# Transposing token chunks and DFT matrices by DMA instead of on TensorE

## The chip, the cores and the metric

The kernel runs on one core of a Trainium2 chip. The metric is device time in microseconds (us) of one execution; lower is better.

## What is computed

A long convolution (H3) is gated by the normalised input, and multiplied by an activated two-layer network of the same input. S = 2048 tokens, D = 640 channels, F = 1728 hidden units, all inputs bfloat16:

```python
x = A_q                                    # 2048 x 640
xn = layernorm(x)                          # no scale, no shift
k_shift = causal 4-tap convolution of A_k along the tokens, a filter per channel
kv = k_shift * A_v
y = irfft(rfft(pad(kv)) * rfft(pad(A_ssm_k)))[:2048]     # per channel
y = y + kv * A_ssm_D
s = xn * y
h = gelu(xn @ B_w1 + B_b1)                 # 2048 x 1728
g = silu(h @ B_w2 + B_b2)
out = x + s * g
```

## The kernel before

**Tokens.** Token 16 p + j lies on partition p, row j. The 16 rows are four chunks of four rows (512 tokens each). Each chunk of x is loaded into a tile `xn` of 128 x 4 x 640, normalised in place, and turned into `xnT`, with channels on the partitions (5 blocks of 128) and 512 tokens along the free dimension. There is one tile `xnT`, used by the four chunks in turn.

**Network.** `ffn1` (L376) makes one of 14 blocks of 128 hidden units for a chunk: five matmuls of 128 x 512 with a block of `w1_sb` stationary and `xnT` moving; `ffn1_out` applies gelu on ACT into `hT`. Steps h0 to h13 are the first chunk, h14 to h27 the second, h28 to h41 the third, h42 to h55 the fourth. `ffn2` (L394) takes a row of a chunk and half of the channels: 14 matmuls of 128 x 320; silu on ACT, and a product into `xn` on DVE. Steps g0 to g31.

**Convolution.** The transform along the tokens is done as matrix products in two factors. `WA` and `WB` (128 x 16 x 128) hold the forward matrices of the first factor, made by sines on ACT (L237); the small ones lie in `mats`. The filter goes through `k_tr` (L421), `k_f1` (kf) with WA and WB, a store to `scrK` in HBM, a load in another order (`kin_load`, fl) and `k_f2` (ff), into `Khat`. The taps and the product with v (`kv_step`, cv) run on DVE; the result goes through `u_f1` (uf), a store to `scrU`, a load (`uin_load`, ml) and `u_f2` (mu). Then come the product with Khat on DVE (`product`, mp), which also needs a half-swapped copy of Khat made by an on-chip DMA (`swap_load`, mk), the first inverse factor (`inv1`, mc), a store to `scrC`, a load (`cab_load`, yl), and the second inverse factor (`inv2`, y). `inv2` multiplies with `GA` and `GB`: `WA` and `WB` with each of their 16 blocks of 128 x 128 transposed. `gate` and `out_add` finish a row.

**The transposes.** The first chunk is transposed in the prologue, block by block on TensorE (L655 to L658), and copied from PSUM to `xnT` by three DVE copies and one of ACT (L659 to L661). The other three use steps `tt` (`x_tr`, L367) and `te` (`x_tr_out`, L373): one `tt` is four matmuls with the identity, one `te` one copy of 128 x 512 from PSUM on ACT or DVE. There are 15 pairs, tt5 to tt9 for the second chunk, tt10 to tt14 for the third, tt15 to tt19 for the fourth. The matrices use `it` (`i2_tr`, L488; eight blocks each, four steps) and `ie` (`i2_out`, L493). The PSUM tiles of `tt` are two buffers that they share with ffn1 and ffn2; those of `it` are three buffers shared with the rest of the convolution.

**Order.** The whole program after the prologue is a list written out in `PLAN` (L30 to L71), a step a word; the letter behind a dot is the engine of a copy (a for ACT, d for DVE). Each engine, and each DMA queue, runs its part of that list in order. Loads, and the swaps of Khat, are issued by SP; stores to scrK, scrU, scrC and most of the output by POOL. So a load on SP waits behind all earlier loads, and a wait of an earlier one holds it back too.

Places that the change touches, in the words of `PLAN` before:

```
... kc3.d kf5 ke5.a ks2 V2 tt7 te7.a kt5 kc5.d tt9 te9.a kt4 gm5 ... K2 tt8 te8.a ... tt5 te5.d tt6 te6.a uf1 kt7 ...
... fl11 uf26 ue26.a cv57 ... fl12 ff16 fe16.d ff17 fe17.a fl15 ff12 fe12.a tt12 te12.a ff14 ...
... mk15 h40 he40 mc21 ... h41 he41 te17.d mc24 ... ms7 q0 g17 ...
```

V and K load four rows of v and of k, q a chunk of x for the last addition.

Of the kernel before, what the change touches and what calls it, by code (L numbers as in the profile page):

```python
# [11 lines left out]
BF16 = mybir.dt.bfloat16  # L12
# [4 lines left out]
P = 128  # L17
# [4 lines left out]
DT = D // P  # L22
# [19 lines left out]
ke28.a h21 he21 uf6 ue6.a kf29 ke29.a ks14 uf7 ue7.a us3 h22 he22 h23 he23 kf26 ke26.a gm7 cv37 cv38 cv41 cv42
cv39 kf27 ke27.a ks13 kt15 kc15.d kf30 ke30.a kf31 ke31.a ks15 fl0 fl1 fl2 h24 he24 fl4 uf10 ue10.a gm6 ls15 ls8
ls9 uf8 ue8.a ls14 uf11 ue11.a us5 h25 he25 h26 he26 uf14 ue14.a cv43 ls13 lv3 lr3 h27 he27 cv44 ls11 lv2 lr2
cv45 cv46 cv47 uf12 ue12.a uf9 ue9.a us4 fl3 uf15 ue15.a us7 g8 ge8 gm8 ln13 ln9 uf13 ue13.a us6 fl5 g9 ge9 ff3
fe3.a ln12 ff1 fe1.d ln10 ff2 fe2.a cv56 ff0 fe0.a cv48 cv49 cv50 ln8 uf21 uf20 ue20.a ue21.a us10 ff8 fe8.a
ln11 g10 ge10 uf16 ue16.a ff6 fe6.d gm9 ff9 fe9.a fl7 ff5 fe5.a ff7 fe7.a fl9 ff4 fe4.a fl8 uf17 ue17.a us8 g11
ge11 cv51 cv52 cv53 cv54 cv55 ff11 fe11.a ff10 fe10.a fl6 uf18 ue18.d uf19 ue19.a us9 fl11 uf26 ue26.a cv57 cv58
cv59 uf24 ue24.a uf27 ue27.a us13 uf25 ue25.a us12 fl12 ff16 fe16.d ff17 fe17.a fl15 ff12 fe12.a tt12 te12.a
ff14 fe14.a cv60 cv61 cv62 cv63 ff18 fe18.a ff15 fe15.a fl13 g12 ff19 fe19.a fl10 uf22 ue22.d ff13 fe13.a fl14  # L50
uf31 gm11 ge12 uf30 ue30.a ue31.d us15 ff23 fe23.d gm12 uf23 ue23.a us11 gm10 tt14 te14.d uf29 uf28 ue28.d
ue29.a us14 mk0 ml0 ml1 mk1 mk2 mk3 ml2 ml3 ml5 ml4 ff31 fe31.a tt13 te13.a tt10 te10.d it0 ie0.d ff27 fe27.d
ff25 fe25.d g13 ge13 gm13 g14 ge14 gm14 ff29 fe29.d ln14 ff28 fe28.a ff24 fe24.d g15 ge15 gm15 ff21 fe21.a tt11
te11.d ff22 fe22.a mu0 mp0 ff26 fe26.a ml7 h28 he28 mu2 mp2 ml10 ml8 mu1 mp1 mk4 mc0 me0.a h29 he29 ff30 fe30.a
mu3 mp3 mk5 ml12 h30 he30 ml11 mc2 me2.a mu4 mp4 mc1 me1.a ms0 mu5 mp5 mk6 h31 he31 ml6 ff20 fe20.a mc3 me3.a
ms1 ln15 mu6 mp6 mc4 me4.a mu7 mp7 mk7 ml9 h32 he32 mu8 mp8 mc5 me5.a ms2 mc6 me6.a mu11 mp11 mc7 me7.a ms3 mu10
mp10 h33 he33 mu9 mp9 mk8 mk9 mc8 me8.a mc10 me10.a mu12 mp12 mu13 mp13 mk10 mc11 me11.a ms5 ml14 h34 he34 ml15
mc12 me12.a it1 ie1.d mc13 me13.a ms6 mu15 mp15 h35 he35 mu14 mp14 mk11 ml13 mc9 me9.a ms4 mu18 mp18 h36 he36
mc14 me14.a mu17 mp17 h37 he37 mu16 mp16 mk12 mc15 me15.a mu20 mp20 h38 he38 mu19 mp19 mk13 mc18 me18.a h39 he39
mu21 mp21 mk14 mc16 me16.a tt17 mc19 me19.a ms9 mc17 me17.a ms8 mu23 mp23 mc20 me20.a mu22 mp22 mk15 h40 he40  # L60
mc21 me21.a ms10 mu24 mp24 mu25 mp25 mc22 me22.a h41 he41 te17.d mc24 me24.a mu26 mp26 mc25 me25.a ms12 tt15
te15.a mu27 mp27 tt16 te16.d mc23 me23.a ms11 mc26 me26.a tt18 te18.d mu29 mp29 it3 ie3.a mu28 mp28 g16 ge16
gm16 mc27 me27.a ms13 it2 ie2.d tt19 te19.a mu31 mp31 mu30 mp30 ms7 q0 g17 ge17 gm17 mc28 me28.a mc31 mc29
me29.d ms14 mc30 me30.d me31.d ms15 yl5 yl2 yl0 yl4 yl3 yl1 yl6 yl11 yl15 q1 g18 ge18 gm18 g19 ge19 gm19 g20
ge20 gm20 g21 ge21 gm21 g22 ge22 gm22 g23 ge23 gm23 h42 he42 h43 he43 y0 yt0 yo0 h44 he44 h45 he45 h46 he46 y5
yt5 yl8 y4 yt4 yo4 yo5 ys2 y1 yt1 yo1 ys0 y3 yt3 h47 he47 h48 he48 h49 he49 h50 he50 h51 he51 y2 yt2 yl7 yl14
yl9 yl10 yl12 yo2 yo3 ys1 q2 h52 he52 h53 he53 h54 he54 h55 he55 y6 yt6 yl13 yo6 y7 yt7 yo7 ys3 q3 y8 yt8 yo8
y11 yt11 g24 ge24 g25 ge25 g26 y12 yt12 gm24 ge26 gm25 ga24 ga25 gs25 y15 yt15 g27 ge27 y14 yt14 y13 yt13 gm26
ga26 gm27 ga27 gs27 y9 yt9 yo9 ys4 y10 yt10 yo10 yo11 ys5 g28 ge28 gm28 ga28 g29 ge29 gm29 ga29 g30 ge30 gm30
ga30 gs30 g31 ge31 gm31 ga31 gs29 gs31  # L70
"""  # L71


# [1 line left out]
def kernel(  # L75
# [15 lines left out]
    nc = tc.nc  # L91

    CH = 4
# [15 lines left out]
    ffnp = ctx.enter_context(tc.tile_pool(name="ffnp", bufs=1))  # L109
# [23 lines left out]
    def evac(eng, out_ap, in_ap):  # L133
        if eng == "a":
            return nc.scalar.copy(out=out_ap, in_=in_ap)  # L135
        return nc.vector.tensor_copy(out=out_ap, in_=in_ap)

    w1_sb = wts.tile([P, DT, FT * P], BF16, name="w1_sb")
# [7 lines left out]
    ident = consts.tile([P, P], BF16, name="ident")  # L146
# [5 lines left out]
    WA = consts.tile([P, NJ, P], BF16, name="WA")  # L152
    WB = consts.tile([P, NJ, P], BF16, name="WB")
    GA = consts.tile([P, NJ, P], BF16, name="GA")
    GB = consts.tile([P, NJ, P], BF16, name="GB")
# [90 lines left out]
    sm = {}  # L246
# [62 lines left out]
                                 rhs=ident[:, h * 64:(h + 1) * 64], start=True, stop=True)  # L309
        return ps  # L310

    xnT = ffnp.tile([P, DT, CH * P], BF16, name="xnT")
    hT = ffnp.tile([P, FT, CH * P], BF16, name="hT")
    kvtmp = ep.tile([P, KC, D], BF16, name="kvtmp")
    live = {}
# [7 lines left out]
    def big_of(key, bf=False):  # L323
        return take(key, ps_big, [P, 1024] if bf else [P, 2, 512], BF16 if bf else F32, "big")

    def ffn_of(key, bf=False):
        return take(key, ps_ffn, [P, 1024] if bf else [P, 512], BF16 if bf else F32, "ffn")
# [36 lines left out]
        nc.vector.tensor_scalar(out=xr, in0=xr, scalar1=live["mv", c][:, j, 0:1], scalar2=live["rs", c][:, j:j + 1],  # L364
                                op0=ALU.subtract, op1=ALU.mult)

    def x_tr(i):  # L367
        c, t = divmod(i, DT)
        tp = ffn_of(("tt", i), True)
        for q in range(CH):  # L370
            nc.tensor.transpose(out=tp[:, q * P:(q + 1) * P], in_=xn_tiles[c][:, q, t * P:(t + 1) * P], identity=ident[:])

    def x_tr_out(i, eng):  # L373
        evac(eng, xnT[:, i % DT, :], live["tt", i][:, 0:CH * P])

    def ffn1(i):  # L376
        ft = i % FT
        ps = ffn_of(("h", i))
        for t in range(DT):
            nc.tensor.matmul(out=ps[:, :], lhsT=w1_sb[:, t, ft * P:(ft + 1) * P], rhs=xnT[:, t, :],  # L380
                             start=(t == 0), stop=(t == DT - 1))

    def ffn1_out(i):
# [101 lines left out]
    def k_f2_out(g, eng):  # L485
        cast(eng, Khat[:, g, :], live["ff", g])

    def i2_tr(i):  # L488
        tp = big_of(("it", i), True)
        for q in range(8):  # L490
            nc.tensor.transpose(out=tp[:, q * P:(q + 1) * P], in_=(WA, WB)[i // 2][:, i % 2 * 8 + q, :], identity=ident[:])

    def i2_out(i, eng):  # L493
        q4 = i % 2
        evac(eng, (GA, GB)[i // 2][:, q4 * 8:(q4 + 1) * 8, :].rearrange("p a b -> p (a b)"), live["it", i][:])

    def add_d():
        nc.vector.tensor_tensor(out=kf_sb[:, :, 0], in0=kf_sb[:, :, 0], in1=dD_sb[:], op=ALU.add)
# [74 lines left out]
    def prologue():  # L573
# [83 lines left out]
                    nc.tensor.transpose(out=tp_of[t][:, q * P:(q + 1) * P], in_=xn[:, q, t * P:(t + 1) * P],  # L657
                                        identity=ident[:])  # L658
        for t in range(DT - 2):  # L659
            evac("d", xnT[:, t, :], tp_of[t])  # L660
        evac("a", xnT[:, DT - 2:DT, :].rearrange("p a b -> p (a b)"), tps[DT - 2][:])  # L661

    steps = {
        "P": load_params, "pt": param_tr, "pb": param_out, "X": load_x, "A": load_w1, "B": load_w2, "C": load_kf, "K": load_k, "V": load_v,
        "ls": ln_stats, "lv": ln_eps, "lr": ln_root, "ln": ln_norm, "tt": x_tr, "te": x_tr_out,
        "h": ffn1, "he": ffn1_out, "g": ffn2, "ge": ffn2_silu, "gm": ffn2_mul, "ga": last_add, "gs": last_store,
        "w": f1_phase, "ws": f1_sines, "d": add_d, "em": tap3, "ee": tap3_out,
        "sp": small_iotas, "s": small_phase, "ss": small_sine, "sm": small_mats,
        "kt": k_tr, "kc": k_tr_out, "kf": k_f1, "ke": k_f1_out, "ks": k_store,
        "cv": kv_step, "uf": u_f1, "ue": u_f1_out, "us": u_store,  # L670
        "fl": kin_load, "ff": k_f2, "fe": k_f2_out, "it": i2_tr, "ie": i2_out,
        "ml": uin_load, "mk": swap_load, "mu": u_f2, "mp": product, "mc": inv1, "me": inv1_out, "ms": c_store,
        "q": xq_load, "yl": cab_load, "y": inv2, "yt": gate, "yo": out_add, "ys": out_store,
    }
# [35 lines left out]
```

## Time and profile before

| What | Value |
|---|---|
| runs | 229.15, 231.75 and 233.93 us, median 231.75 |
| profiled execution, first to last instruction | 231.0 us |
| its mean granted TensorE clock | 0.984 |
| TensorE (PE) busy | 211.6 us, 1420 matmuls |
| DVE, ACT, POOL busy | 184.1, 149.6, 43.1 us |
| DMA | 57.61 MB, 25209 packets |
| 60 matmuls and 15 copies of `tt`/`te` | PE 5.46, ACT 4.70, DVE 2.85 us busy |
| 32 matmuls and 4 copies of `it`/`ie` | PE 2.44, DVE 2.08, ACT 1.01 us busy |

The profile is of one execution; its own time, apart from the span, is not listed among the runs, and the span lies 0.75 us below their median. PE is TensorE's matmuls, PEld its weight loads, DVE VectorE, ACT ScalarE, POOL GpSimd, SP SyncE, which computes nothing here and issues DMAs. A row of a group gives line, engine, operation, output and inputs with shapes, and count; then busy us and mean ns of one; then the engine's idle time just before them. Matmuls overlap: one can last 219 ns while the next begins after 55 ns. The chain is the work that ended last, followed back from the end; its pieces have a start and a length in us. DMA issues are given with their size and the median time from issue to landing.

### The profile page before, as it was taken

Reading aid. Unit: us, or ns where it says so; the run is one execution under the profiler, and the core shown is the slowest. Engines: PE = TensorE matmul, PEld = TensorE weight load, DVE = VectorE, ACT = ScalarE, POOL = GpSimd, SP = SyncE. Lnnn points to the kernel's source line nnn. Section 1 sums busy time; section 2 is a strip of 40 time slices with the busy share of each in tenths; the row PEclk is TensorE's granted clock in tenths of the full one; section 3 lists DMA queues with packets and bytes.
Section 4 is the critical chain, followed back from the end, with each engine's and each line's share of the span. In section 5 each row is a group of like instructions: output and inputs, shape, how many; then the busy total and the mean of one; then the engine's idle time right before and its main releaser. Section 6 shows DMA issues by size and latency. Waiting matters only on the chain.

```text
span 231.0 us, 3921 instructions
## 1 busy us (share of the span) xinstructions
PE 211.6 (92%) x1420; PEld 131.7 (57%) x1420; DVE 184.1 (80%) x315; ACT 149.6 (65%) x232; POOL 43.1 (19%) x75
## 2 busy tenths in 40 slices
PE   7859999899999899979999965999999999999993
PEld 4524456677555556646765532556677765457772
DVE  7799999889989999999779885699998115444892
ACT  3934687998988999898468742567782244562111
POOL 8100020042232344120200220212222000100010
PEclk9988999999999999999999997999999999999999
DMA  7999995654844479599779999877943695379323
GB/s 219 349 380 355 409 413 206 191 209 174 305 191 188 179 236 381 176 309 337 266 215 294 303 353 295 257 231 188 270 156 131 207 340 200 150 218 367 124 89 114
DMA packets 25209, 57.61 MB, mean 249 GB/s; under 512 B 2854, under 2 KB 14055, under 8 KB 25190
## 3 DMA queue, kind: packets, MB, share of 16 engines
q1 hardware_dynamic: 20726, 39.66, 52.6%
q0 software_dynamic: 4320, 17.70, 20.5%
q8 instruction: 11, 0.18, 0.3%
q14 instruction: 8, 0.07, 0.1%
q10 hardware_dynamic: 144, 0.01, 0.0%
HBM read 33.76 MB, written 18.35 MB: 226 GB/s over the span
## 4 chain that ended last, share of the span: by engine, by line
PE 65%; ACT 12%; DMA 9%; DVE 8%; issue 3%; SPq 1%; DVEq 0%; ACTq 0%
PE g L399 22%; PE h L380 21%; ACT Khat L135 6%; DMA kh<-scrU 6%; PE uf L340 3%; PE mc L537 3%; DMA Khat<-Khat 3%; PE mc L538 2%; PE mu L340 2%; PE kf L340 2%; PE ff L340 2%; PE y L556 2%; PE y L557 2%; DMA skp<-in_A_shift_k_dram 1%; ACT sl L404 1%
## 5 line engine op out<-in xcount | busy, mean ns | idle before, releaser
L380 PE MATMUL h<-xnT,w_sb 128*128 128x512 bf16 x280 | 68.4, 390 | 1.5 <-ACT hT L386 1.2
L399 PE MATMUL g<-w_sb,hT 128*128 128x320 bf16 x448 | 63.7, 299 | 0.6 <-ACT sl L404 0.6
L386 ACT ACTIVATE hT<-h,b_f 128x512 bf16<-128x512 f32 (+1 forms) x56 | 38.3, 690 | 27.3 <-PE h L380 24.2
L399 PEld LDWEIGHTS <-hT 128*128 128x128 bf16 x448 | 43.8, 98 | 18.1 <-issue 0.8
L529 DVE TENSOR_TENSOR p<-mu,Khat 128x1280 bf16<-128x1280 f32 x32 | 45.8, 1484 | 5.4 <-PE mu L340 3.7
L380 PEld LDWEIGHTS <-w_sb 128*128 128x128 bf16 x280 | 27.9, 100 | 31.3 <-issue 4.6
L404 ACT ACTIVATE sl<-g 128x320 bf16<-128x320 f32 x32 | 13.9, 439 | 36.1 <-PE g L399 32.5
L135 ACT CAST c<-mc 128x640 bf16<-128x640 f32 x29 | 19.9, 692 | 8.6 <-PE mc L538 7.9
L544 POOL DMA_DIRECT2D scrC<-c x16 | 11.5, 718 | 56.0 <-ACT c L135 51.8
L409 DVE TENSOR_TENSOR xn<-xn,sl 128x320 bf16<-128x320 bf16 x32 | 10.1, 322 | 14.0 <-ACT sl L404 13.8
L472 DVE TENSOR_TENSOR uc<-uc,kvtmp 128x1280 bf16<-128x1280 bf16 x24 | 19.8, 824 | 0.7
L476 DVE TENSOR_TENSOR kvtmp<-kh,w_exp 128x1280 bf16<-128x1280 bf16 x24 | 19.7, 820 | 0.5
L340 PEld LDWEIGHTS <-mats 128*128 128x128 bf16 x128 | 12.1, 97 | 13.8 <-issue 4.9
L537 PE MATMUL mc<-p,mats 128*128 128x320 bf16 x64 | 18.6, 305 | 1.2 <-DVE p L529 0.7
L538 PE MATMUL mc<-p,mats 128*128 128x320 bf16 x64 | 18.5, 304 | 0.0
L563 DVE TENSOR_TENSOR t<-y,xn 128x640 bf16<-128x640 f32 x12 | 9.8, 820 | 10.4 <-PE y L557 10.3
L135 ACT CAST Khat<-uf 128x640 bf16<-128x640 f32 x26 | 17.0, 697 | 0.4 <-PE uf L340 0.4
L340 PE MATMUL mu<-kh,mats 128*128 128x320 bf16 x64 | 13.5, 300 | 3.7 <-DMA kh<-scrU 2.5
L135 ACT CAST Khat<-ff 128x640 bf16<-128x640 f32 x24 | 15.5, 699 | 0.5 <-PE ff L340 0.4
L135 ACT CAST Khat<-kf 128x640 bf16<-128x640 f32 x22 | 15.1, 711 | 0.3 <-PE kf L340 0.2
L440 POOL DMA_DIRECT2D scrK<-Khat x16 | 8.9, 554 | 31.2 <-ACT Khat L135 16.6
L340 PE MATMUL ff<-kin,mats 128*128 128x320 bf16 x64 | 12.3, 298 | 1.4 <-ACT Khat L135 1.3
(111 smaller groups left out, 269.4 us busy)
## 6 DMA issues: line engine op xcount, KB each, us to landing
scrK<-Khat POOLq DMA_DIRECT2D x16, 320.0 KB, 2.6
scrU<-Khat POOLq DMA_DIRECT2D x16, 320.0 KB, 4.2
kin<-scrK SPq DMA_DIRECT2D x16, 320.0 KB, 4.6
Khat<-Khat SPq DMA_DIRECT2D x32, 160.0 KB, 4.2
kh<-scrU SPq DMA_DIRECT2D x16, 320.0 KB, 5.4
scrC<-c POOLq DMA_DIRECT2D x16, 320.0 KB, 3.9
kh<-scrC SPq DMA_DIRECT2D x16, 320.0 KB, 6.2
kh<-in_A_k_dram SPq DMA_DIRECT2D x4, 640.0 KB, 6.1
```

What stands on the lines that cost most here:

```text
L135: return nc.scalar.copy(out=out_ap, in_=in_ap)
L340: nc.tensor.matmul(out=ps[:, h, 0:HALF], lhsT=lhsT, rhs=rhs[:, h * HALF:(h + 1) * HALF], start=start, stop=stop)
L380: nc.tensor.matmul(out=ps[:, :], lhsT=w1_sb[:, t, ft * P:(ft + 1) * P], rhs=xnT[:, t, :], start=(t == 0), stop=(t == DT - 1))
L386: nc.scalar.activation(out=hT[0:M, ft, :], in_=live["h", i][0:M, :], func=ACT.Gelu_apprx_tanh, bias=b1_f[0:M, ft:ft + 1], scale=1.0)
L399: nc.tensor.matmul(out=ps[:, 0:HALF], lhsT=hT[0:M, ft, q * P:(q + 1) * P], rhs=w2_sb[0:M, ft, hs], start=(ft == 0), stop=(ft == FT - 1))
L404: nc.scalar.activation(out=sl[:], in_=live["g", i][:, 0:HALF], func=ACT.Silu)
L472: nc.vector.tensor_tensor(out=uc[:], in0=uc[:], in1=kvtmp[:], op=ALU.add)
L476: nc.vector.tensor_tensor(out=(kvtmp if s else uc)[:], in0=kh[:, r0:r0 + KC, :], in1=w_exp[:, j:j + 1, :].to_broadcast([P, KC, D]), op=ALU ...
L529: nc.vector.tensor_tensor(out=p[:].rearrange("p k (h c) -> p k h c", h=2), in0=live["mu", g][:, None, :, 0:HALF].to_broadcast([P, 2, 2, HA ...
L537: nc.tensor.matmul(out=psC[:, h, 0:HALF], lhsT=I1a, rhs=p[:, 0, hs], start=True, stop=False)
L538: nc.tensor.matmul(out=psC[:, h, 0:HALF], lhsT=I1b, rhs=p[:, 1, hs], start=False, stop=True)
L544: nc.gpsimd.dma_start(out=pair_view(scrC)[g2], in_=live["c", g2][:])
```

## The change

Steps `tt`, `te`, `it` and `ie` are removed from `PLAN`, with their functions. Each of the second to fourth chunk is turned by one transposing DMA on SP (`xd1`, `xd2`, `xd3`), and each of the two matrices by one (`ig0`, `ig1`). The first chunk stays on TensorE. The two inner dimensions of `xnT` change places, since the DMA turns row after row: it is now 128 x 4 x 5 x 128 (row, block of channels, token), and ffn1 reads it in four runs of 128.

```diff
-    xnT = ffnp.tile([P, DT, CH * P], BF16, name="xnT")
+    xnT = ffnp.tile([P, CH, DT, P], BF16, name="xnT")
...
-    def x_tr(i):
-        c, t = divmod(i, DT)
-        tp = ffn_of(("tt", i), True)
-        for q in range(CH):
-            nc.tensor.transpose(out=tp[:, q * P:(q + 1) * P], in_=xn_tiles[c][:, q, t * P:(t + 1) * P], identity=ident[:])
-
-    def x_tr_out(i, eng):
-        evac(eng, xnT[:, i % DT, :], live["tt", i][:, 0:CH * P])
+    def x_turn(c):
+        nc.sync.dma_start_transpose(out=xnT[:].rearrange("p q t s -> p (q t) s"),
+                                    in_=xn_tiles[c][:].rearrange("p q d -> p (q d)"))
...
-            nc.tensor.matmul(out=ps[:, :], lhsT=w1_sb[:, t, ft * P:(ft + 1) * P], rhs=xnT[:, t, :],
+            nc.tensor.matmul(out=ps[:, :], lhsT=w1_sb[:, t, ft * P:(ft + 1) * P], rhs=xnT[:, :, t, :],
...
-    def i2_tr(i):
-        tp = big_of(("it", i), True)
-        for q in range(8):
-            nc.tensor.transpose(out=tp[:, q * P:(q + 1) * P], in_=(WA, WB)[i // 2][:, i % 2 * 8 + q, :], identity=ident[:])
-
-    def i2_out(i, eng):
-        q4 = i % 2
-        evac(eng, (GA, GB)[i // 2][:, q4 * 8:(q4 + 1) * 8, :].rearrange("p a b -> p (a b)"), live["it", i][:])
+    def i2_turn(i):
+        nc.sync.dma_start_transpose(out=(GA, GB)[i][:], in_=(WA, WB)[i][:].rearrange("p n r -> p (n r)"))
...
-            evac("d", xnT[:, t, :], tp_of[t])
-        evac("a", xnT[:, DT - 2:DT, :].rearrange("p a b -> p (a b)"), tps[DT - 2][:])
+            evac("d", xnT[:, :, t, :], tp_of[t].rearrange("p (q s) -> p q s", q=CH))
+        evac("a", xnT[:, :, DT - 2:DT, :].rearrange("p q t s -> p t q s"), tps[DT - 2][:].rearrange("p (t q s) -> p t q s", t=2, q=CH))
```

In `PLAN` the new steps stand here; the order of all others is as before:

```
... kc3.d kf5 ke5.a ks2 xd1 V2 kt5 kc5.d kt4 gm5 ...
... fl11 xd2 uf26 ue26.a cv57 ...
... mk15 ig0 ig1 h40 he40 mc21 ... h41 he41 xd3 mc24 ... ms7 q0 g17 ...
```

## Prediction

> **What bounds the kernel now.** I read the shares of the page first, then the busy times by stage, then the rows of the work that goes, then the chain of waits and the order of time around each place where a transposing DMA enters, and last the DMA rows.
>
> ```profile
> PE 211.6 (92%) x1420; PEld 131.7 (57%) x1420; DVE 184.1 (80%) x315; ACT 149.6 (65%) x232; POOL 43.1 (19%) x75
> PE 65%; ACT 12%; DMA 9%; DVE 8%; issue 3%; SPq 1%; DVEq 0%; ACTq 0%
> ```
>
> The first line is the busy time of each engine over the span, the second the chain that ended last, by engine. By stage:
>
> ```profile
> 44.00:57.00 13.00, 12.45 (x115) 9.52 (x115) 10.86 (x22) 12.26 (x23) 3.75 (x7) 1.00 0.60 220
> ...
> 100.00:120.00 20.00, 18.65 (x143) 12.59 (x141) 16.61 (x29) 13.98 (x25) 3.25 (x6) 1.00 0.83 276
> ...
> 133.00:143.00 10.00, 5.71 (x31) 3.04 (x30) 6.82 (x5) 3.28 (x5) 1.43 (x2) 0.95 1.05 339
> 143.00:163.00 20.00, 19.79 (x122) 11.40 (x120) 17.68 (x14) 12.79 (x19) 3.90 (x6) 0.94 0.80 231
> 163.00:176.00 13.00, 12.93 (x110) 9.35 (x109) 12.45 (x14) 9.46 (x14) 3.25 (x5) 1.00 0.63 206
> ```
>
> After the stretch (us from the start) the columns are its length, then the busy time of PE, PEld, DVE, ACT and POOL, the clock and the DMA share. PE is the bound over most of the span, and it is full from 143 on. ACT is nearly as full from 44 to 57. Only 133 to 143 leaves PE idle (5.71 of 10 us busy), and there the DMA share is 1.05: the kernel waits for loads.
>
> **What is removed.** These rows go:
>
> ```profile
> L371 PE MATMUL tt<-ident,xn 128*128 128x128 bf16 x60 | 5.5, 219 | 0.0
> L135 ACT COPY xnT<-tt 128x512 bf16<-128x512 bf16 x8 | 4.7, 609 | 0.0
> L136 DVE COPY xnT<-tt 128x512 bf16<-128x512 bf16 x7 | 2.8, 419 | 0.0
> L491 PE MATMUL it<-ident,WA 128*128 128x128 bf16 x16 | 1.2, 219 | 0.0
> ```
>
> 219 ns is the time of one matmul, but they overlap. What PE really gives is read from the chain, which counts each stretch once:
>
> ```profile
> 103.20 0.22 PE tt L371 x4
> ...
> 110.44 0.45 PE tt L371 x8
> 110.89 0.45 PE it L491 x8
> ...
> 118.93 1.19 ACT Khat L135 x2
> ...
> 126.99 5.86 DMA Khat<-Khat
> ```
>
> Four transposes are 0.22 us and eight of the DFT matrices 0.45 us. So 15 x 0.22 + 4 x 0.45 = 5.1 us of PE go, with 4.7 + 1.0 us of copies on ACT and 2.8 + 2.1 us on DVE. By place:
> - 44 to 57 (chunk 1): 5 x 0.22 = 1.1 us of PE and 2.34 us of four ACT copies, with both engines over 94% busy. The chain here changes between ACT and PE; I take 1.3 us, between the 1.1 of PE and the 2.3 of ACT.
> - 100 to 120 (chunk 2, and the first half of one matrix): the chain holds 0.22 + 0.22 + 0.45 + 0.45 = 1.3 us. All of that lies ahead of the DMA piece at 126.99, so the waiting stage moves forward as a whole. The fifth group, at 118.57, is not on the chain: nothing.
> - 143 to 176 (chunk 3, three matrix halves): PE is 32.7 of 33 us busy. 5 x 0.22 + 3 x 0.45 = 2.45 us of PE go; I take 2.2, as DVE (30.1 of 33) is close behind and loses 2.5 us of its own.
> Together 1.3 + 1.3 + 2.2 = 4.8 us, if all transposes are hidden.
>
> **What is added.** Five transposing DMAs on SP: three of 640 KB (20 blocks of 128x128) and two of 512 KB (16 blocks). Nothing is moved on POOL, and the order of the other instructions of each engine stays. No row of this trace shows a transposing DMA. These are the nearest ones (KB each, median us to landing):
>
> ```profile
> kh<-in_A_k_dram SPq DMA_DIRECT2D x4, 640.0 KB, 6.1
> vc<-in_A_v_dram SPq DMA_DIRECT2D x4, 640.0 KB, 7.7
> Khat<-Khat SPq DMA_DIRECT2D x32, 160.0 KB, 4.2
> q1 hardware_dynamic: 20726, 39.66, 52.6%
> ```
>
> Call t the time for which one 640 KB transpose holds SP and the transfers behind it, and t + 2.5 the time to landing; 2.5 us is the shortest landing of a 160 KB on-chip copy. From below, SP holds a plain issue for 0.33 to 0.6 us and 640 KB land in 6.1: t = 3.6. From above, each source row of a block (128 elements, 256 bytes) costs a packet of the mean length: 0.526 x 231 x 16 / 20726 = 94 ns, so 2560 x 94 ns / 16 = 15 us. I take t = 5.2, from the dearest plain load of the same size (7.7 - 2.5), the nearest row; a 16-block one costs 0.8 t. The ends 3.6 and 15 stay for the range.
>
> The Trainium skill has rules on both sides. Its page "Advanced Engine Details and Errata", section "X-Bar Transpose (TRN2)", says that transposing DMAs run about as fast as regular ones, which is near the lower end. Its page "VectorE: DVE Perf Modes", section "The three transpose paths", gives 1309 ns for one 128x128 block by DMA against 390 ns on TensorE, where this trace has about 55 ns (0.22 / 4) on TensorE. An estimate by that page, block after block, is 20 x 1.309 = 26 us for a chunk; no run here shows it yet.
>
> Now the three places.
> - Chunk 1. The DMA stands ahead of the third load of v and of k on SP and waits for the last normalisation:
>
> ```profile
> 45.80 0.44 DVE L364 TENSOR_SCALAR xn<-xn,mv,rs 128x640 bf16<-128x640 bf16 x1
> ...
> 57.09 1.24 PE L380 MATMUL h<-xnT,w_sb 128*128 128x512 bf16 x5
> ...
> 61.51 0.82 DVE L476 TENSOR_TENSOR uc<-kh,w_exp 128x1280 bf16<-128x1280 bf16 x1
> ```
>
> It starts at 46.2 and lands at 53.9; the first matmul that reads it is due at 57.1 - 1.3 = 55.8. Hidden up to t = 7. The two loads went at 41.2 and 41.6 before; now they go at 46.2 + 5.2, and k lands 6.1 later, at 57.9, where DVE wants it at about 60.2. Also hidden, up to t = 7.5.
> - Chunk 2. The DMA goes at 100, after the eleventh kin load (99.57); five kin loads wait behind it. The next stood at 101.38, so they are late by t - 1.4 = 3.8. The second of them (kin 15, about 101.7 plus 4.6) is read at 110.0: less the issue and landing, slack of 3.0. 0.8 us is lost, and each us of t above 4.4 is lost here. The DMA share is 0.99 from 104 to 109.7, so no free bandwidth helps. The transpose itself has over 40 us to land, as its reader runs at 143.
> - Chunk 3 and the matrices. The first matrix goes when the swap loads end, at 163.2 before, 160.5 now. Then 0.8 t + 0.8 t + t = 2.6 t = 13.5, to 174.0; landed at 176.5. The third DMA's wait for the last matmul of chunk 2 (164.05 before) is over by then. Readers: chunk 3's matmuls, at 188.0 before and about 183.5 now. Behind the DMAs stand the loads of scrC, at 181.80 before and about 178 now; the first product that reads one has 1 us to spare. Hidden up to 2.6 t = 18.5, t = 7.1.
>
> xnT also gets another layout, so a 512-wide moving operand is read in four runs of 128. The warm-up matmuls, which read the identity in four runs, take 379 ns at the least and those on xnT 376: nothing, and at the outside 3 ns x 280 = 0.8 us.
>
> Sum: 231.0 - 4.8 + 0.8 = 227.0 us of span. The median of the runs is 0.75 us above the profiled span (231.75 against 231.0); with that, 227.8.
>
> **The rivals.**
> - All hidden, chunk 2's loads too (t at most 4.4): 231.0 - 4.8 + 0.75 = 226.95, so 227.0. For it speaks that on-chip copies land early; against it that SP must place far more pieces than for a plain load.
> - The transposes hold SP for longer, and become the wait. Slower, by one mechanism: the queue time t. At t = 9 chunk 1 loses 1.9, chunk 2 4.6, and the loads of scrC start at 160.5 + 23.4 = 183.9 against 179, 4.9: 231.75 - 4.8 + 11.4 = 238.4. It decides from t = 7.6 on, where the losses (0.5 + 3.2 + 1.3) reach the 4.8. For it: 2560 rows of 256 bytes each. Against it: the DMA queue of ACT moved 144 packets of less than 100 bytes in a share that the page rounds to 0.0%.
> - The same with packets at the mean price (t = 15): 7.9 + 10.6 + 20.5 lost, 231.75 - 4.8 + 39.0 = 266. By the 1309 ns a block that the page "VectorE: DVE Perf Modes" of the Trainium skill gives, with t = 26, the estimate would be 18.9 + 21.6 + 49.1 lost, about 317.
> - The gain is lost in the DMA stage: the 1.3 us of 100 to 120 come to nothing because 121 to 144 is full of transfers (1.04 and 1.05), and the 1.3 MB that chunk 2's transpose reads and writes at a share of 0.94 to 0.99 push them back by 2 us (0.66 MB at the 336 GB/s of that stretch): 227.8 + 1.3 + 2 = 231.1, no change.
>
> **Chances.** Forecast and the fully hidden rival (t up to 7): 0.47, of which 0.25 below 227.1 and 0.22 above it. Gain lost in the DMA stage: 0.13. t of 7 to 11 (230 to 247): 0.21, of which 0.06 under 236.4. t above 11: 0.19. A measurement of this kernel can tell about 2% from no change, which is 227.1 and 236.4. So faster 0.25, same 0.22 + 0.13 + 0.06 = 0.41, slower 0.15 + 0.19 = 0.34. The likeliest case's own range is 226.3 (all 5.1 of PE, and 0.3 more from ACT) to 230; the range that leaves out no more than 2 in 10 is 226 to 247.
>
> **What would show it.** Right: transposing DMAs that land in 6 to 9 us and hold SP for some 5; no wait of PE for xnT, GA or GB; a wait for kin of about 1 us near 108; PE's 5.46 + 2.44 us busy on the transposes gone; the stage after 143 shorter by about 2.2 us. Wrong: SP held for 8 us or more at 46 and three times in a row after 160, with PE waiting for xnT at 57 and before chunk 3, and the scrC loads after 182. The matmuls on xnT at over 380 ns would show the layout costing something. The forecast is wrong if t is outside 3.6 to 7, as most places are hidden only inside it.

## The result, and the profile after

The changed kernel takes 242.68 us (median of 4 runs, 240.63 to 243.02), the kernel before in the same sitting 230.89 (4 runs, 229.15 to 233.93): a ratio of 1.052 with a 95% interval of 1.044 to 1.061. It is slower by 5%. The time lies inside the range of the prediction, 226 to 247, but 14.9 us above the forecast of 227.8, and on the other side of the kernel before. The profiled execution took 242.37 us, with a span of 240.2. Here and below, the ratios leave out executions more than 1.5% above the quickest of the same kernel, so a ratio can lie below that of the medians beside it.

From the page of the changed kernel: the busy times, the packets of all queues, SP's queue (packets, MB, share), and the chain by engine:

```profile
PE 210.6 (88%) x1328; PEld 127.4 (53%) x1328; DVE 180.3 (75%) x305; ACT 145.2 (60%) x223; POOL 42.9 (18%) x75
...
DMA packets 37143, 60.60 MB, mean 252 GB/s; under 512 B 14790, under 2 KB 25991, under 8 KB 37126
...
q1 hardware_dynamic: 32662, 42.67, 60.5%
...
PE 51%; DMA 20%; ACT 12%; DVE 7%; issue 5%; SPq 2%; POOL 0%; DVEq 0%; ACTq 0%; POOLq 0%
```

The instructions are gone as planned (1328 matmuls for 1420). In their place the chain has 20% of DMA where it had 9%, and SP's queue 11936 more packets, nearly all of 256 bytes: 3 x 2560 + 2 x 2048 = 11776. Their mean price follows from the queue's busy share: (0.605 x 240.2 - 0.526 x 231.0) x 16 engines / 11936 = 32 ns each, so one chunk's 2560 packets fill all 16 engines for 5.1 us in the mean. The places differ: the packet records of the trace give 22 ns a packet during the first transpose, as in a transpose alone (e5), and 45 ns during the second.

The busy times by stage, columns as in the prediction:

```profile
44.00:57.00 13.00, 9.85 (x79) 6.96 (x80) 8.79 (x18) 9.69 (x17) 3.44 (x6) 1.00 0.73 191
100.00:120.00 20.00, 14.11 (x81) 7.87 (x80) 14.66 (x21) 13.79 (x23) 3.61 (x7) 0.88 1.07 257
133.00:143.00 10.00, 9.35 (x56) 5.24 (x54) 8.38 (x7) 7.50 (x12) 1.71 (x3) 1.00 1.03 314
143.00:163.00 20.00, 16.08 (x86) 8.79 (x86) 15.69 (x11) 9.40 (x15) 3.31 (x5) 0.91 0.92 285
163.00:176.00 13.00, 12.36 (x76) 7.24 (x75) 12.22 (x10) 8.89 (x14) 2.80 (x4) 1.00 0.85 216
```

Where chunk 1 and chunk 2 are turned, all engines now have idle time: PE 9.85 of 13 us and ACT 9.69 (12.45 and 12.26 before), PE 14.11 of 20 (18.65). At the second place the granted clock fell to 0.88 as well.

Five points that every kernel here passes cut the span into stages: a, from the start to the first matmul of kf; b, from there to the first of ff (chunk 1 is turned in it); c, to the first product on DVE (chunk 2); d, to the end of the last product; e, to the first matmul of y (last chunk and matrices); f, to the end. All in us, from the order of time of each profile:

| kernel | a | b | c | d | e | f | span |
|---|---|---|---|---|---|---|---|
| before | 44.1 | 44.5 | 31.0 | 55.9 | 14.8 | 40.8 | 231.0 |
| after | 44.5 | **48.4** | **35.9** | 54.3 | **16.1** | 41.0 | 240.2 |
| e1 chunk 1 only | 45.0 | **48.6** | 31.0 | 55.8 | 14.8 | 41.1 | 236.1 |
| e2 chunk 2 only | 44.4 | 44.4 | **36.9** | 57.4 | 14.8 | 40.8 | 238.7 |
| e3 chunk 3 and matrices | 43.9 | 44.4 | 31.0 | 57.3 | 15.7 | 41.5 | 233.8 |
| e4 layout only | 44.4 | 44.4 | 31.0 | 53.7 | 14.8 | 40.9 | 229.2 |
| e6 unused transposes | 42.8 | **48.8** | **36.7** | 54.1 | 14.8 | 40.7 | 237.9 |
| e7 unused copies in pieces | 44.5 | **48.1** | 31.5 | 53.8 | 14.8 | 40.7 | 233.3 |
| e8 chunk 1, ten buffers | 45.1 | 44.2 | 31.0 | 55.0 | 14.8 | 40.8 | 230.9 |
| e9 all, more buffers | 45.0 | 44.2 | **40.1** | 50.1 | 15.9 | 41.1 | 236.4 |
| e10 before, more buffers | 42.8 | 44.3 | 31.4 | 54.3 | 14.8 | 40.9 | 228.4 |
| e11 matrices early | 43.5 | **51.2** | 31.8 | 54.2 | 15.0 | 40.8 | 236.4 |
| e12 all, places moved | 44.3 | **50.6** | **36.0** | 54.6 | 15.2 | 41.1 | 241.9 |
| e13 chunk 2, more buffers | 45.0 | 44.3 | **39.8** | 51.1 | 14.8 | 40.8 | 235.7 |
| e14 chunk 2 behind kin | 42.5 | 44.3 | **33.7** | 55.4 | 14.8 | 40.9 | 231.7 |
| e15 all but chunk 2, more buffers | 44.1 | 44.2 | 31.3 | 54.1 | **21.8** | 41.3 | 236.9 |
| e16 all, chunk 2 behind kin | 45.1 | 44.2 | **33.4** | 56.1 | 15.4 | 41.1 | 235.3 |
| e17 chunks left out | 42.8 | 44.3 | 30.7 | 53.9 | 14.8 | 40.9 | 227.3 |
| e18 all left out | 44.8 | 44.3 | 30.5 | 55.8 | 15.3 | 40.9 | 231.5 |

Stages a and d vary by 2 to 3 us between kernels that do the same in them, in part with the granted clock (a is 42.8 us in e10 and e17, where it is 1.00 from 6 us on, and 44.1 in the kernel before, where it is 0.96); b, c, e and f repeat within half a us. So the 9.2 us between the two spans are 3.9 in b, 4.9 in c, 1.3 in e, 0.6 in a and f, less 1.6 in d, which is within what d varies by. The medians lie 11.8 us apart. Most of the rest lies in the execution that was profiled: the kernel before takes 1.7 to 1.9 us longer than its span in each of its executions, so the profiled one took an estimated 232.7 us, 1.8 above the median of 230.89.

SP's queue of the changed kernel, its transposing DMAs in order of time (start, time that SP is held), with the five loads of kin behind the second:

```profile
46.82 4.27 SPq L367 DMA_TRANSPOSE xnT<-xn  x1
...
104.34 6.19 SPq L367 DMA_TRANSPOSE xnT<-xn  x1
110.62 3.42 SPq L474 DMA_DIRECT2D kin<-scrK  x5
...
171.94 4.73 SPq L483 DMA_TRANSPOSE GA<-WA  x1
176.77 3.85 SPq L483 DMA_TRANSPOSE GB<-WB  x1
180.72 6.04 SPq L367 DMA_TRANSPOSE xnT<-xn  x1
```

SP is held for 4.3 to 6.2 us by a chunk, about the t = 5.2 of the prediction. What it did not see are these waits, new in the window from 44 to 64 (us in total, times, longest):

```profile
DVE Khat L135 <- DMA scrK<-Khat: 2.4, 1, 2.4
ACT Khat L134 <- DMA scrK<-Khat: 2.3, 2, 1.9
```

and in the window from 100 to 126:

```profile
PE uf L339 <- DVE Khat L135: 3.6, 1, 3.6
...
DVE Khat L135 <- DMA scrU<-Khat: 3.2, 1, 3.2
ACT Khat L134 <- DMA scrU<-Khat: 2.7, 1, 2.7
PEld L339 <- DMA kin<-scrK: 1.8, 2, 1.1
...
PE ff L339 <- DMA kin<-scrK: 0.7, 2, 0.5
```

The results of kf and uf are copied from PSUM into four buffers (rows of Khat that are filled last, `Ring`), and POOL stores them from there. A copy waits until the store of four results ago has landed. The landing of the stores of scrK in the window 44 to 66, before:

```profile
DMA to landing us min/median/max: 2.4/2.6/3.2
```

and after:

```profile
DMA to landing us min/median/max: 2.9/6.1/8.1
```

POOL's queue was not touched, yet its stores land up to 5 us later while the transpose beside them runs. DVE and ACT then wait to copy, PE waits for them.

In the chain, the longest pieces of 100 to 126 and of the time around the last product (start, length) are a load of kin that stood behind the second transpose, and the last store of scrC:

```profile
112.35 7.23 DMA kin<-scrK
...
187.02 6.34 DMA scrC<-c
```

The five loads of kin landed in 6.8 to 7.6 us (5.2 to 5.9 before), the last two stores of scrC in 6.1 to 6.3 (the last ones before in 2.8 to 3.3).

### The profile page after: what moved, and what is told of

Same layout as the page of the kernel before. It is cut to its first block, busy times and chain, and to the rows that moved or that the text cites. A ratio compares the mean times of both kernels' runs of the same rounds, so it can differ in the third digit from the quotient of the medians.

```text
span 240.2 us, 3725 instructions
## 1 busy us (share of the span) xinstructions
PE 210.6 (88%) x1328; PEld 127.4 (53%) x1328; DVE 180.3 (75%) x305; ACT 145.2 (60%) x223; POOL 42.9 (18%) x75
## 4 chain that ended last, share of the span: by engine, by line
PE 51%; DMA 20%; ACT 12%; DVE 7%; issue 5%; SPq 2%; POOL 0%; DVEq 0%; ACTq 0%; POOLq 0%
PE h L374 19%; PE g L393 15%; ACT Khat L134 5%; DMA prm<-in_B_b_dram 4%; DMA scrK<-Khat 3%; DMA kh<-scrU 3%; DMA kin<-scrK 3%; DVE p L517 3%; DMA scrC<-c 3%; PE mu L339 2%; PE mc L525 2%; PE uf L339 2%; PE kf L339 2%; DMA kh<-scrC 2%; PE mc L526 2%
## 5 line engine op out<-in xcount | busy, mean ns | idle before, releaser
L393 PEld LDWEIGHTS <-hT 128*128 128x128 bf16 x448 | 44.1, 98 | 18.6 <-issue 0.8
L532 POOL DMA_DIRECT2D scrC<-c x16 | 11.4, 715 | 56.1 <-ACT c L134 51.9
L403 DVE TENSOR_TENSOR xn<-xn,sl 128x320 bf16<-128x320 bf16 x32 | 10.1, 321 | 14.9 <-ACT sl L398 14.7
L525 PE MATMUL mc<-p,mats 128*128 128x320 bf16 x64 | 18.3, 301 | 1.9 <-DVE p L517 0.8
L526 PE MATMUL mc<-p,mats 128*128 128x320 bf16 x64 | 18.2, 299 | 0.0
L134 ACT CAST Khat<-ff 128x640 bf16<-128x640 f32 x24 | 15.4, 696 | 1.7 <-PE ff L339 1.6
L339 PE MATMUL ff<-kin,mats 128*128 128x320 bf16 x64 | 13.0, 313 | 2.4 <-ACT Khat L134 1.8
```

The lines of the kernel that those rows point to most:

```text
L339: nc.tensor.matmul(out=ps[:, h, 0:HALF], lhsT=lhsT, rhs=rhs[:, h * HALF:(h + 1) * HALF], start=start, stop=stop)
L393: nc.tensor.matmul(out=ps[:, 0:HALF], lhsT=hT[0:M, ft, q * P:(q + 1) * P], rhs=w2_sb[0:M, ft, hs], start=(ft == 0), stop=(ft == FT - 1))
L525: nc.tensor.matmul(out=psC[:, h, 0:HALF], lhsT=I1a, rhs=p[:, 0, hs], start=True, stop=False)
L526: nc.tensor.matmul(out=psC[:, h, 0:HALF], lhsT=I1b, rhs=p[:, 1, hs], start=False, stop=True)
L532: nc.gpsimd.dma_start(out=pair_view(scrC)[g2], in_=live["c", g2][:])
```

## The experiments

Theory A: a transpose puts thousands of 256-byte packets into the DMA engines, and stores and loads of every queue beside it land late; the engines wait for a buffer or for a load. Theory B: what stands behind the transpose on SP is late, as the prediction had it. Theory C: xnT is late or its layout slow. All kernels keep the new layout of xnT where a chunk is turned by DMA.

**e1, e2, e3, e4: the change in parts.** From the kernel before, with the steps taken out and put in as in the change:

```diff
e1: - tt5..tt9 te5..te9                     + ... ks2 xd1 V2 ...
e2: - tt10..tt14 te10..te14                 + ... fl11 xd2 uf26 ...
e3: - tt15..tt19 te15..te19 it0..it3 ie0..ie3   + ... mk15 ig0 ig1 h40 ... xd3 mc24 ...
e4: the layout of xnT alone, all transposes on TensorE
```

> Only the second chunk is turned by DMA; the other two and the matrices stay on TensorE, with the new layout of xnT. Theory A (the transposing DMA fills the DMA engines for some 10 us, so the stores to scrK beside it land late, and the copies that need their four buffers wait): about 3.9 us slower than before, with landings of scrK of up to 8 us and waits of ACT and DVE for them. Theory B (loads that are queued behind it on SP come late): slower too, but with DVE waiting for the third load of k. Theory C (the transposed chunk itself lands late): PE waits for xnT. If the change only loses in chunk 2 and later: 1.3 us faster.

> Only the third chunk is turned by DMA, with the new layout. Theory A (late stores to scrU hold back copies): about 4.6 us slower than before, with landings of scrU of up to 10 us. Theory B (five kin loads late behind it on SP): also slower, but with PE waiting for kin for 3 us or more and no wait for scrU. If the loss came from chunk 1 alone: 1.3 us faster.

> Only the fourth chunk and the two matrices are turned by DMA, with the new layout. Theory A: few transfers stand beside them, so about 1 us faster than before (2.2 us of PE work go, the last scrC stores land late). Theory B and C: 0 to 2 us slower, as the three together hold SP for 15 us and the loads of scrC start late.

> All transposes stay on TensorE; only the layout of xnT is the new one. Theories A to C: no change, within 0.5 us of before. If four runs of 128 cost the matmuls or the copies something: slower by 1 us or more, with matmuls on xnT above 379 ns.

Measured, as ratios to the kernel before with their intervals: e1 237.31 us, 1.025 (1.012 to 1.037); e2 237.13, 1.025 (1.014 to 1.037); e3 234.28, 1.004 (0.998 to 1.010); e4 232.29, 1.003 (0.997 to 1.009). Chunk 1 costs 4.1 us in stage b, chunk 2 5.9 in c (in a profiled execution of 240.48 us; the other three took 235.97 to 238.04). e4 shows the layout to cost nothing: the matmuls on xnT stay at 376 ns at the least, 379 in the median, and PE hardly waits for xnT in any kernel, so theory C falls. e3 brings neither the 2.2 us that the prediction had for this part nor a loss clear of the spread, though the median of all its runs is 1.1% above that of the kernel before (231.63).

**e5: the transfers by themselves.** A kernel of its own that computes nothing of the reference: a 640 KB tile is turned by DMA, copied on the chip in 256-byte pieces (into every second block of a tile twice as wide), or copied in whole rows, each alone and each with three 320 KB stores from POOL beside it.

```diff
+ nc.sync.dma_start_transpose(out=turned[:], in_=x[:].rearrange("p a b -> p (a b)"))
+ nc.sync.dma_start(out=spread[:, :, 0:P], in_=x[:])
+ nc.sync.dma_start(out=whole[:], in_=x[:])
+ nc.gpsimd.dma_start(out=keep[i], in_=st[:])   # i = 0, 1, 2, beside each of the above, and alone
```

> A kernel of its own that computes nothing of the reference: 640 KB on chip are moved from one tile to another as a transposing DMA, as a plain copy in 2560 pieces of 256 bytes and as a plain copy in rows of 5 KB, each alone, then each with three stores of 320 KB from POOL beside it, then each with a load of 320 KB behind it on SP; DVE waits for all landings between the stages. Theory A (the price is the crossbar: its blocks hold all DMA engines): the transposing DMA alone lands in some 8 us where the plain ones take 4 to 5, and the stores beside it land 4 us or more later than alone. Theory A2 (the price is the 256-byte pieces): the plain copy in pieces is as slow and delays the stores as much. Theory B (only the queue of SP is held): stores from POOL land as if alone, and only the load behind it is late.

| us to landing | alone | with three stores beside | these stores |
|---|---|---|---|
| transpose, 20 blocks | 4.9 | 8.9 | 6.2, 7.1, 7.4 |
| copy in 256-byte pieces | 4.8 | 6.6 | 2.5, 5.9, 6.2 |
| copy in whole rows | 3.2 | 4.2 | 3.2, 4.4, 4.8 |
| the stores alone | | | 2.5, 2.9, 3.2 |

The table goes by the order of time, as the waits of DVE let each group of stores run one step earlier than the program lists it. In a second round of the same transfers the transpose landed in 4.9 us alone and 8.3 beside the stores, and these in 3.4, 6.6 and 6.9. SP is held for 3.2 us by the transpose alone, 0.7 by the pieces, 0.5 by the whole rows. So beside the transpose the stores land some 4 us late (the first one in the second round only 0.9); plain pieces of the same size do most of that without any transposing; but only the transpose holds SP. A load behind it on SP went 3.9 us after it, when the queue was free, and then landed in 3.3 us (3.4 alone). The Trainium skill, page "Advanced Engine Details and Errata", section "X-Bar Transpose (TRN2)", has transposing DMAs as fast as regular ones: here 4.9 us against 3.2 for whole rows, and equal only to a copy in pieces. The 1309 ns of the Trainium skill, page "VectorE: DVE Perf Modes", section "The three transpose paths", are for one block. Block after block, as in the estimate of 26 us, they do not hold here: 4.9 us for 20 blocks is 245 ns each; a single block was not measured.

**e6, e7: one suspected cost added.** The kernel before, whole, with two unused transfers of 512 KB at the places of xd1 and xd2: transposes in e6, copies in 256-byte pieces in e7.

```diff
+ e6: nc.sync.dma_start_transpose(out=extra_of(c), in_=xn_tiles[c][:]...[:, 0:NJ * P])
+ e7: nc.sync.dma_start(out=extra_of(c), in_=xn_tiles[c][:]... in 16 pieces of P)
... ks2 xd1 V2 ...  fl11 xd2 uf26 ...
```

> The kernel before with all its TensorE transposes, and two transposing DMAs of 512 KB more, at the places of those of chunks 1 and 2, into tiles that nobody reads. Theory A: 6 to 8 us slower (0.8 of 3.9 + 4.6, and the 1.3 + 1.3 us of TensorE work not saved), with late stores. Theory C (the turned data come late): no change, since nobody waits for them.

> As the last, but the two extra DMAs are plain on-chip copies of the same 512 KB in pieces of 256 bytes. Theory A (crossbar): at most 2 us slower. Theory A2 (small pieces): as slow as with the two extra transposing DMAs, 6 to 8 us.

e6 took 239.23 us, 7.3 over the 231.93 of the kernel before on that chip (four runs, 234.51 to 239.74); e7 236.86 with one run of 313.67 among its four, and without that run a ratio of 1.023 (1.015 to 1.031). No transposition is taken from TensorE here, so this is the price of the transfers alone. The stages part the two theories: in b the pieces cost 3.6 us and the transposes 4.3, almost the same; in c the pieces 0.5 and the transposes 5.7. Chunk 1 is theory A, chunk 2 has theory B in it. SP's queue at the second place, e6:

```profile
103.08 4.43 SPq L381 DMA_TRANSPOSE GB<-xn  x1
107.60 4.27 SPq L487 DMA_DIRECT2D kin<-scrK  x5
```

and e7:

```profile
104.05 0.62 SPq L381 DMA_DIRECT2D GB<-xn  x1
105.41 6.79 SPq L488 DMA_DIRECT2D kin<-scrK  x5
```

**e8, e9, e10: more buffers.** The wait for stores is taken away by giving their results more room: rows of Khat that are not filled yet. e8 is e1 with ten buffers in place of four for the first 24 results; e9 the whole change and e10 the kernel before, both with more buffers for the first 28.

```diff
+    class WideRing(Ring):
+        def tile(self, *_, **__):
+            free = [NG + 2 * i for i in range(NR // 2)]
+            if self.n < 24:
+                free += [NG // 2 + 2 * i for i in range(6)]
+            r0 = free[self.n % len(free)]
...
-    pools["ring"] = Ring(Khat, NG, NR // 2)
+    pools["ring"] = WideRing(Khat, NG, NR // 2)
```

> Only the second chunk is turned by DMA, as in the first experiment, but the first 24 results that are stored to scrK and scrU go round ten buffers instead of four, in rows of Khat that are free then. Theory A (late stores matter because copies wait for a free buffer): the loss of 2.5% shrinks to less than 1%, and no wait for scrK is left. Theory B or C: still 2% or more slower.

> The changed kernel as it is, but the results that are stored to scrK and scrU go round ten buffers for the first 24 and have four more for the next four, in rows of Khat that are free then. Theory A (late stores hurt because copies wait for one of four buffers): the loss falls from 5% to 1 or 2%; what is left is kin late by some 2 us in chunk 2 and the late scrC loads. Theory B (SP's queue, late loads) or C: still 4 to 5% slower.

> The kernel before with the same additional buffers and no transposing DMA: no theory expects a change (within 0.5%), as no copy waits for a store there. If it is faster by 2% or more, the additional buffers are worth something by themselves, and the experiments with them show less.

e8: 233.2 us, 1.005 (1.000 to 1.010). e10: 231.3, 0.999 (0.993 to 1.005). The stores of e8 land as late as in e1, in the window 44 to 66:

```profile
DMA to landing us min/median/max: 3.0/6.0/8.0
```

but nothing waits for them, and stage b is back at 44.2. With the control e10 this settles chunk 1: late stores and four buffers cost all that b had lost. It also shows that the hidden transpose brings nothing: 44.2 against 44.3 in e10, not 1.3 us less. e9 still takes 238.21, 1.031 (1.023 to 1.040): stage b is mended, c is worse, at 40.1.

**e11, e12: other places.** e11 has the buffers of e10 and turns only the matrices by DMA, at 71 us, where the DMA share is about 0.5 in e10; e12 is e9 with that, and with chunk 2 turned ahead of g10.

```diff
e11: - it0..it3 ie0..ie3      + ... ks12 ig0 ig1 kt13 ...
e12: after, more buffers:  ig0 ig1 ahead of kt13; xd2 from ahead of uf26 to ahead of g10
```

> Chunks on TensorE as before; only the two matrices are turned by DMA, and early, ahead of the step kt13, where SP issues nothing else (some 75 us); with the additional buffers. Theory A: 0.3 to 1.5 us faster than before (1.8 us of TensorE and 2 us of DVE work go; late stores hold nobody up). Theory B: no change, SP is idle there.

> The changed kernel with the additional buffers, the matrices turned early as in the last, and the third chunk turned some 6 us earlier, ahead of step g10, so that its kin loads are not queued behind it when they are due. Theory A: within 1% of before. Theory B: the loss of chunk 1 stays, 2% slower.

Both miss: e11 238.83 us, 1.028 (1.019 to 1.036), e12 242.33, 1.044 (1.033 to 1.055). The place looked quiet, and was not: the last stores of scrK run there, and all loads of kin wait for the last one. The five stores of scrK in e11 from 70 to 90 (2.4 to 2.6, median 2.5, in e10):

```profile
DMA to landing us min/median/max: 3.5/7.3/9.0
```

The last is issued at 78.96 and lands 9.0 us later; the first load of kin goes at 88.06, against 80.90 in e10. The waits from 84 to 100, and PE, DVE and ACT in stretches of 2 us (busy time, clock, DMA share):

```profile
PEld L339 <- DMA kin<-scrK: 7.1, 1, 7.1
PE ff L339 <- DMA kin<-scrK: 6.7, 1, 6.7
```

```profile
90.00:92.00 2.00, 0.00 (x0) 0.00 (x0) 0.00 (x0) 0.00 (x0) 0.00 (x0) 0.79 0.86 302
92.00:94.00 2.00, 0.00 (x0) 0.00 (x0) 0.00 (x0) 0.00 (x0) 0.00 (x0) 0.50 0.95 337
94.00:96.00 2.00, 1.29 (x5) 0.74 (x6) 0.01 (x1) 0.54 (x1) 0.00 (x0) 0.50 1.06 384
96.00:98.00 2.00, 1.75 (x7) 0.85 (x6) 2.00 (x4) 1.44 (x3) 0.00 (x0) 0.51 0.36 124
98.00:100.00 2.00, 2.00 (x16) 1.46 (x15) 1.97 (x3) 1.61 (x3) 0.03 (x1) 1.00 0.00 0
```

All engines stand still for some 6 us because of a store. The columns also show a second price: after the pause the clock is granted at 0.50 until about 98. In e12, c is 36.0 as well: ahead of g10, ten loads of kin stand behind xd2 instead of five, and PE waits for kin for 3.2 us from 100 to 132.

**e13 to e16: what is left of e9.** All with the buffers of e10. e13: only chunk 2, at the change's place. e14: the same with xd2 behind the last load of kin. e15: the whole change but chunk 2. e16: the whole change, with xd2 as in e14.

```diff
e13: ... fl11 xd2 uf26 ...                          (five loads of kin behind it)
e14, e16: ... fl14 xd2 uf31 ...                     (none behind it)
e15: tt10..tt14 te10..te14 stay; xd1, ig0 ig1, xd3 as in the change
```

> The kernel before with the new layout and the buffers of e10, and only the second of the moved chunks turned by DMA, at the changed kernel's place: ahead of five loads of kin. e2 did this with four buffers and took 1.025 times the kernel before. If what is left of the whole change (e9, 1.031) is chunk 2's, here by the loads of kin that stand behind the transpose and land late under it: 1.015 to 1.03, with waits of PE for kin of 4 us or more and next to none for stores of scrU. If the buffers were what chunk 2 suffered from as well: 0.995 to 1.005, no such wait over 2 us.

> As e13, but the transpose goes behind the last load of kin instead of ahead of five of them, near 107 us, some 12 us ahead of the first matmul that reads it (118.8 in e10). If the queue is what costs (loads of kin standing behind 6 us of transpose): the waits for kin are gone, the first matmul on xnT waits up to 2 us, and the time is 1.00 to 1.01. If any transpose here costs because its packets fill the DMA engines, whatever stands behind it: 1.015 to 1.03 again, with the waits now for the swapped rows of Khat, for the loads of kh, or for xnT itself.

> The whole change with the buffers of e10, apart from chunk 2, which stays on TensorE. If chunk 2 is nearly all that was left in e9: 1.00 to 1.01, the sum of e8 (1.005) and e3 (1.004). If the tail costs more once the earlier stages are quick: 1.015 to 1.025, with a longer time from the last product to the first output transform (16.3 us before, 17.6 in the changed kernel) and later loads of scrC.

> The whole change with the buffers of e10 and chunk 2's transpose behind the last load of kin. If the parts add up, it takes e15 plus what e14 loses: 1.005 to 1.02 by the queue theory, 1.025 to 1.04 by the other. Under 1.00 would mean that the removed TensorE work pays at last, which neither theory expects.

e13: 237.06 us, 1.026 (1.014 to 1.038). e14: 234.12, 1.015 (1.006 to 1.025). e15: 234.89, 1.017 (1.007 to 1.028). e16: 237.49, 1.028 (1.017 to 1.039). Waits of e13 from 100 to 126:

```profile
PEld L339 <- DMA kin<-scrK: 8.2, 4, 5.4
PE ff L339 <- DMA kin<-scrK: 5.4, 2, 5.1
```

and of e14:

```profile
PE mu L339 <- DMA kh<-scrU: 2.8, 1, 2.8
PEld L339 <- DMA kin<-scrK: 0.7, 1, 0.7
PE ff L339 <- DMA kin<-scrK: 0.4, 1, 0.4
```

More buffers don't help chunk 2 (e13 against e2); taking the loads of kin out from behind the transpose does: c falls from 39.8 to 33.7. The rest of 2.3 us over e10 lies where the loads of kh now land late. So in c the queue is the larger part and the traffic the smaller one, which fits the 0.5 us of e7's pieces; the place of the transpose also moved by 5 us, so the two are not parted cleanly. In the whole time e13 and e14 are only 2.9 us apart, and their intervals overlap. In the whole change (e16 against e9) c falls by as much, from 40.1 to 33.4, yet the medians are close, 237.49 and 238.21, since d, 56.1 against 50.1, gives 6 us of it back. A first product that comes 8 to 9 us late finds its loads landed, and d is then shorter; this was read from e9 and e13, not tried by itself. e15 is nearer the second of its two expectations. Its profiled execution (238.82 us; the other three took 233.13 to 234.97) shows the mechanism of chunk 1 once more, in the tail: the 16 stores of scrC, the last ones beside the three transposes,

```profile
  ACT c L134: 4.9, 1
...
DMA to landing us min/median/max: 3.2/5.6/11.8
```

take up to 11.8 us to land, and a copy of c waits 4.9 us for its buffer. In the changed kernel the latest took 9.7 us (7.7 before). How much of e15's 1.7% is that, and how much is spread, stays open.

**e17, e18: the gain by itself.** Work is left out and nothing put in its place: in e17 the transposes of the second to fourth chunk with their copies (ffn1 reads the first chunk's tokens for all), in e18 those of the matrices too (`inv2` reads WA and WB).

```diff
e17: - tt5..tt19 te5..te19
e18: - tt5..tt19 te5..te19 it0..it3 ie0..ie3
-            nc.tensor.matmul(out=psY[:, h, 0:HALF], lhsT=GA[:, n2, :], rhs=cab[:, 0, hs], start=True, stop=False)
+            nc.tensor.matmul(out=psY[:, h, 0:HALF], lhsT=WA[:, n2, :], rhs=cab[:, 0, hs], start=True, stop=False)
```

> The kernel before with the new layout, and the transposes of the second to fourth chunk with their copies left out, nothing in their place: ffn1 of these chunks reads the first chunk's tokens again, so the output is another one. If the prediction's gain terms are right (1.3 for chunk 1, 0.9 of the 1.3 for chunk 2, 1.1 of the 2.2 for chunk 3): about 3.3 us faster, 0.986. If the removed work lay in waits of other engines, as the stages of e8 say for chunk 1 (0.1 us from the first kf to the first ff): 0.995 to 1.000, with 44.3 us from the first kf to the first ff against 44.45 before and 31.0 from there to the first product.

> As e17, and the transposes of the two DFT matrices and their copies are left out as well; the output transform reads the matrices as they were before turning, so the output is another one. This is all the work that the change takes from TensorE, ACT and DVE, with nothing put on the DMA queues. By the prediction's gain terms: 4.8 us faster, 0.979. If the removed work lay in waits: 0.99 to 1.00, and then no placement of transposing DMAs could have made this kernel faster by more than that.

e17: 231.25 us, 0.998 (0.993 to 1.003). e18: 231.96, 0.998 (0.991 to 1.004), 12 runs each. The page of e18 shows that the work is gone:

```profile
PE 209.8 (91%) x1328; PEld 127.5 (55%) x1328; DVE 180.1 (78%) x305; ACT 144.7 (63%) x223; POOL 43.1 (19%) x75
...
PE 62%; DMA 13%; ACT 13%; DVE 6%; issue 3%; SPq 1%; DVEq 0%; ACTq 0%; POOLq 0%
```

In b it brings 0.2 us, in c 0.5. By the ratio, all that the change takes away is worth 0.5 us (0.2% of 232), at most 2.1 by the interval, and by the medians of all runs nothing (231.96 against 231.68); the 4.8 of the prediction is excluded. Even DMAs that cost nothing could not have brought it.

## Why the prediction was wrong, point by point

- **The gain of 4.8 us** (1.3 + 1.3 + 2.2). Wrong: e18 has 0.5 at the likeliest, which cannot be told from nothing. The step that failed is the reading of the chain and of the busy shares. A piece on the chain was taken as time that goes with it. In b, where 1.3 us were forecast, e8 and e17 have 0.1 to 0.2. The chain before held 0.45 us of tt and 0.50 of a copy into xnT from 44 to 58; in e17 they are gone, and kf on PE has 17.4% of the chain there instead of 5.0%. So PE, ACT and DVE hand results to each other, and what one has no more to do is waited out for another; this is read from the chains, not tried. In 143 to 176, PE's 32.7 of 33 us was read as PE being the bound. Without chunk 3's transposes d is 53.9 in e17, and 53.7 to 55.0 in kernels that kept them and had the same clock of 1.00 there (e4, e7, e8, e10).
- **t, the time that SP is held.** Right: 4.27 to 6.19 us for a chunk against 5.2, and 4.73 and 3.85 for a matrix against 0.8 t = 4.2. The upper bound of 15 us, from packets at the mean price of 94 ns, is excluded: they took 32 in the mean. The landing, t + 2.5 = 7.7, was too small beside other traffic: 12.2 us in e2. The sign that the prediction named for being wrong, t outside 3.6 to 7, did not appear: what failed lay beside t.
- **Chunk 1 "hidden up to t = 7".** Wrong, by 3.9 us in b. t was 4.3 and no reader of xnT waited, as forecast. But the step asked only who waits for xnT and for the loads behind the DMA on SP, and said "Nothing is moved on POOL". The step that failed is this list of who can be hurt. The stores on POOL's queue landed late beside the transpose, 2.6 us became 6.1, and four buffers did not cover that (e1 against e8).
- **Chunk 2, loss of 0.8 us.** Wrong by size: 4.9 in c instead of 0.8 less 1.3. Its mechanism, the loads of kin behind the transpose, is there (e13 against e14, 6.1 us with more buffers), but not alone: the loads also land later (6.8 to 7.6 us where the sum had 4.6), the stores of scrU too (copies wait 5.9 us for them), and PE runs at half clock after the pause (0.50 from 116 to 120). The time for the transpose to land was misread as well: its first reader ran at 119.83, not at 143. That slip cost nothing, as PE did not wait for xnT.
- **Chunk 3 and matrices "hidden up to t = 7.1".** Nearly right in size: e3 is unchanged within its interval, and e in the changed kernel 1.3 us longer. But the loads of scrC did not wait for SP, as the prediction had it: SP was free from 188.2, and they went at 193.5, when the last store of scrC had landed (187.02 and 6.34 us). The third transpose left SP's queue at 186.8, 12.8 us after the 174.0 of the prediction: 8.8 that b and c had lost, 2.6 of gain that was not there, and 1.1 by the three holds, 14.6 us for 13.5.
- **The layout: nothing, at the outside 0.8.** Right (e4).
- **The 0.75 us from span to time.** Too small: it set the span of one execution against the median of others. Within an execution of the kernel before it is 1.7 to 1.9 us, so this is 1 us of the 14.9.
- **The rivals.** "The transposes hold SP for longer" came nearest (238.4), for a t of 9 that was not there. The range reached up to 247 for the sake of such a t; that the time lies in it is luck. "The gain is lost in the DMA stage" had the right kind, traffic pushing other traffic, but put it at 121 to 144 and at 2 us. The rival that was missing: stores on another queue land late, and the buffers behind them are few.

## What to carry to other kernels

Before a DMA of many small rows is put into a busy kernel, look at what every queue has in flight beside it, not only its own queue, and ask of each of these transfers how late it may land: how many buffers stand behind a store, and which load waits for the last of a row of stores. A low DMA share is not slack (0.44 to 0.54 in e10 at the place where e11 lost 7 us); the last store before a change of order is on the path even there. And work on a chain where several engines hand over to each other is worth what a kernel with that work left out gains, which is quickly measured, before anything is built to hide it.

## What the runs showed of the hardware

- A 640 KB transpose on the chip lands in 4.9 us alone, as a copy in 256-byte pieces does (4.8), against 3.2 for whole rows; it holds the issuing queue for 3.2 us alone and up to 6.4 beside other traffic (e13; once 9.25, the third in e15), the pieces 0.7.
- Beside it, 320 KB stores of another queue take 6.2 to 7.4 us to land instead of 2.5 to 3.2 (e5; 3.4 to 6.9 in its second round); in the kernels single stores took 8 to 11.8.
- A wait of PE is paid more than once. After a pause of PE of 5.1 us in e13 (111.2 to 116.3), the clock in stretches of 4 us (the column ahead of the DMA share):

```profile
108.00:112.00 4.00, 2.68 (x15) 1.22 (x13) 3.77 (x7) 3.49 (x6) 1.07 (x2) 1.00 1.16 219
112.00:116.00 4.00, 0.00 (x0) 0.00 (x0) 0.04 (x1) 0.00 (x0) 0.54 (x2) 0.65 1.04 383
116.00:120.00 4.00, 2.96 (x16) 1.90 (x17) 1.33 (x2) 0.69 (x1) 0.00 (x0) 0.50 1.07 370
120.00:124.00 4.00, 4.00 (x19) 2.34 (x18) 0.92 (x2) 0.40 (x1) 0.00 (x0) 0.57 1.08 273
124.00:128.00 4.00, 4.00 (x31) 2.87 (x30) 2.36 (x5) 1.16 (x3) 0.00 (x0) 1.00 1.06 239
```

PE works at half clock for 2.96 + about 3.5 us, which costs it about 3 us more than the pause itself. This agrees with the Trainium skill, page "TensorE: Matmul & The Clock Gate", section "Part 1: The HAM clock gate", by which at least one idle window of some 3.4 us halves the clock and at least one busy one restores it: here 5.1 us of pause, and 6.4 of work.
